# Routing's steps behind the passes that begin a pair of chunks, and the logits' products one slot sooner

## The chip, the cores and the metric

The kernel runs on one core of a Trainium2 chip. The metric is the time of one execution on the device in microseconds (us); the time of a kernel is the median of several executions. The engines are called as in the profile: PE (TensorE, matrix products), ACT (ScalarE), DVE (VectorE), POOL (GpSimd) and SP (here only a queue that issues DMAs). Each engine works through its own queue in order and waits on semaphores for the others.

## The reference

Three stages, each feeding the next; 2304 tokens (4 batches of 576) of 512 numbers.

```python
# 1. attention with a threshold, 8 heads of 64
scores = q @ k.T / 8
scores = where(scores >= max(scores) - tau, scores, -1e9)
x = softmax(scores) @ v
# 2. first mixture: a dense layer with a rational function
h = x @ w_in                                   # 512 -> 2048
P = a[0] + a[1]*h + a[2]*h**2 + a[3]*h**3
Q = 1 + abs(b[0])*abs(h) + abs(b[1])*h**2
x = (P / (Q + 1e-6)) @ w_out                   # 2048 -> 512
# 3. second mixture: 8 experts, the best one per token
logits = x @ w_gate
e = argmax(logits, axis=1)
gate = softmax(logits)[e];  eom = sigmoid(x @ w_output_gate)[e]
out = gate * eom * (relu(x @ w1[e]) @ w2[e])   # 512 -> 1024 -> 512
```

## The kernel before

The order of all engines' work is written out by hand: Python loops emit the instructions, and each engine runs its own in the order in which they were emitted.

**The first mixture** (`moe1`) works in slots. In slot `t` the chunk `c = t - 53` is begun: a chunk is 128 of the 2048 hidden columns for three token tiles of 128 (one of the six groups `r`). `emit_in(c)` issues its twelve products into PSUM (L945); two chunks, an even `c` and the odd one behind it, are a pair and share one PSUM tile `hps[p]`, of which there are two. So even `c` stand in odd slots and odd `c` in even slots. In a slot with odd `c` the pair that is complete is taken up by the vector engines, 768 columns at a time. ACT makes `ah` (L968), `s1` (L969) and `t1` (L970); POOL multiplies `t1` by `ah` (L971); DVE has two passes that begin the pair, L973 and L974, which read the pair's PSUM tile. In the next slot ACT makes the quotient as a logarithm and an exponential over the same PSUM tile (L980, L981). In the slot after that, DVE ends the pair with three passes, L959, L960 and L961, ACT writes `gh` (L998) and POOL `gl` (L999). Thus in each even slot DVE has the three last passes of one pair and then the two first of the next.

`emit_out` issues the nine products of the chunk begun five slots earlier with `w_out` (L1017); when a group has all its chunks, the rows are added up (L1047) and written out.

**Fillers.** `emit_in` is given a list `fill` of small pieces of work. `FILL = (0, 0, 9, 0, 0)` says how many of them are emitted behind each of the slot's DVE passes: up to nine behind the third. In a slot that both ends and begins pairs, they so stand between L961 and L973; what is left goes to the slot's end. The decoding of weights (`chains(t)`, until slot 93) and the steps of the first routing (`side.fill(t)`) both come in this list.

**The first routing** (`route(..., first=True)`) ranks the first nine token tiles by expert. It is a generator; each `yield` ends one step, mostly one small DVE instruction, some on ACT (L1446, L1455) or PE (counts L1326/L1328, permutation L1433, scales L1483). `ROUTE_STEPS` says how many steps each slot takes, from slot 127 to slot 152. Two parts of the first experts' work stand beside it: the halving of weights (L1650 on ACT, L1651 on DVE) and eight pieces of a transposition (L1598, L1601, L1602) in slots 141 to 148; L1602 is emitted at the end of a slot's passes ("late").

**The logits.** For a finished group of three tiles, `y_max` (L1071) and a power of two scale it, `y_hi` writes two halves of 16 bits (L1080 on ACT, L1081 on DVE), `y_turn` transposes them by DMA on SP (L1086), `y_logits` multiplies by the gates (L1096, eight products per tile, at the end of a slot's PE work), and `y_fin` (L1103 to L1108) writes the logits. Tile `i` is split and turned in slot `s + 1 + i`, multiplied in slot `s + Y_LOG + i`, and `y_fin` stands one slot behind the last product. The routing's PSUM results and the logits' products share one bank.

What follows the mixture is a loop over expert slots with a second routing in its beginning (`rt` in the names where the first has `temp`).

Of the kernel before, what the change touches and what calls it, by code (L numbers as in the profile page):

```python
# [105 lines left out]
Y_MAX = 0  # L106
Y_HI = 1
Y_TURN = 1
Y_LOG = 4
Y_FIN = 1  # L110
GATES = 44
ROUTE_AT = 9
# [554 lines left out]
def moe1(nc, tc, xT, vs, w_in, w_out, a, bb, w_gate, w_ogate, gates, ident, yd, part, L, consts, keep, side, early_bank):  # L667
# [3 lines left out]
    def pool(name, bufs, **kw):  # L671
        return (psum if "space" in kw else ctx).enter_context(tc.tile_pool(name=name, bufs=bufs, reuse_waits="tile", **kw))
# [21 lines left out]
    def w_cols(lo, n):  # L694
        if n < 4:
            return w4[lo][:, :, n * P:(n + 1) * P]
        return (wih, wil)[lo][:, :, (n - 4) * P:(n - 3) * P]
# [6 lines left out]
    def open_wo():  # L704
        p = right(keep, "wo")
        wo.append([p.tile([P, NFC // 2, DM], F32R, name=x) for x in ("woh", "wol")])
# [4 lines left out]
    def at(slot, f, *args):  # L711
        hooks.setdefault(max(slot, 0), []).append((f, args))
# [3 lines left out]
    def chains(slot):  # L716

        return steps.pop(slot, [])

    def run(slot):  # L720
        order = (load_next, last_bits, exponent, sum_in, red_in, clamp_red, split_out, split_in, scale_in, factors_in)
        for f, args in sorted(hooks.pop(slot, ()), key=lambda x: order.index(x[0]) if x[0] in order else -1 - (x[0] in early)):
            f(*args)
# [137 lines left out]
    for key in STREAM:  # L861
        t = end[key]
# [9 lines left out]
    for m in GROUPS:  # L872
        if n < 2 * m:
            for i in range(n, n + m):
                at(end[0, i] + (i != 2), sum_in, i)
            t = SECOND_SUM if n else EARLY_SUM
# [6 lines left out]
        else:  # L883
            for i in range(n, n + m):
                at(end[0, i] + 1, sum_in, i)
            t = max(end[0, i] for i in range(n, n + m)) + 1
# [33 lines left out]
    def h_tile():  # L920
        return ps_h.tile([P, 2, DM], F32, tag="h", name="h")
# [8 lines left out]
    def buf(tag, bufs, dt=F32, name=None):  # L930
        return m_p.tile([P, 2, n], dt, tag=tag, bufs=bufs, name=name or tag)

    def emit_in(c, fill):

        p, odd = divmod(c, 2)
        ops, late = [], []
        if c < len(chunks):
            j, fc, r = chunks[c]
            t0 = TR * r
            if not odd:  # L940
                hps[p] = h_tile()
            hb = hps[p][:, odd]
            parts = [(0, k, lo) for k in range(4) for lo in range(2)] + [(1, k, 0) for k in range(4)]
            for i, (w, k, lo) in enumerate(parts):
                nc.tensor.matmul(  # L945
                    hb[:, 0:n], w_cols(w, fc)[:, k], xT[:, k, t0:t0 + TR, lo, :],
                    start=(i == 0), stop=(i == 11))
            if spare:
                first, last = spare.pop(0)(hb[:, n:DM])
                if first:  # L950
                    first()
                late.append(last)
        if odd:
            if p - 1 in st:
                q = p - 1
                t, s = st.pop(q)
                x = hps.pop(q)[:, :, 0:n]
                ops += [
                    lambda: stt(t, t, one, x, op0=ALU.add, op1=ALU.mult),  # L959
                    lambda: stt(x, t, 2.0, x, op0=ALU.subtract, op1=ALU.mult),  # L960
                    lambda: (stt(s, s, na0, x, op0=ALU.add, op1=ALU.mult), emit_g(q, s)),  # L961
                ]
            if c < len(chunks):

                hp = hps[p][:, :, 0:n]
                c1, c2, ca1, ca3 = (cvs[:, i, t0 // UT, fc - 1:fc] for i in range(4))
                ah, t1, s1 = buf("ah", 1), buf("t", 3), buf("s", 4)
                nc.scalar.activation(ah, hp, AF.Abs, scale=c1)  # L968
                nc.scalar.activation(s1, hp, AF.Identity, bias=na2, scale=ca3)  # L969
                nc.scalar.activation(t1, ah, AF.Identity, bias=b0, scale=b1)  # L970
                nc.gpsimd.tensor_tensor(t1, t1, ah, op=ALU.mult)  # L971
                ops += [
                    lambda: stt(s1, s1, c2, hp, op0=ALU.mult, op1=ALU.mult),  # L973
                    lambda: stt(s1, s1, ca1, hp, op0=ALU.add, op1=ALU.mult),  # L974
                ]
                st[p] = t1, s1
        elif p - 1 in st:

            x, t = hps[p - 1][:, :, 0:n], st[p - 1][0]
            nc.scalar.activation(x, t, AF.Ln, bias=one)  # L980
            nc.scalar.activation(x, x, AF.Exp, scale=-1.0)  # L981
        ops += late
        if c == 1:
            at(HALVES[0] + 0.5, lambda ops=ops: [f() for f in ops])
            ops = []
        fill = list(fill)
        for f, k in itertools.zip_longest(ops, FILL):
            if f:
                f()
            for _ in range(min(k or 0, len(fill))):  # L990
                fill.pop(0)()
        for f in fill:
            f()

    def emit_g(q, s):

        gh, gl = buf("t", 3, F32R, "gh"), buf("s", 4, F32R, "gl")
        nc.scalar.activation(gh, s, AF.Copy)  # L998
        nc.gpsimd.tensor_tensor(gl, s, gh.bitcast(F32), op=ALU.subtract)  # L999
        for i in range(2):  # L1000
            gs[2 * q + i] = gh[:, i], gl[:, i]
# [4 lines left out]
    def emit_out(c):  # L1006
        j, fc, r = chunks[c]
        gh, gl = gs.pop(c)
        _, (f0, f1), end = SEGS[j]
        first, last = fc == f0, fc == f1 - 1  # L1010
        if first:
            for i in range(TR):
                acc[r, i] = bank(i)
        wh, wl = (x[:, fc % (NFC // 2)] for x in wo[fc // (NFC // 2)])
        for i in range(TR):
            for m, (g, w) in enumerate(((gh, wh), (gh, wl), (gl, wh))):
                nc.tensor.matmul(  # L1017
                    acc[r, i], g[:, i * P:(i + 1) * P], w, start=first and m == 0, stop=last and m == 2)
        if last:
            for i in range(TR):  # L1020
                (part_out if end == 1 else y_out)(r, i)
# [128 lines left out]
    for r in ORDER:  # L1150
# [3 lines left out]
        else:  # L1154
            at(s + Y_MAX, y_max, r)
            for i in range(TR):
                at(s + Y_HI + i, y_hi, TR * r + i)
                at(s + Y_TURN + i, y_turn, TR * r + i)
                at(s + Y_LOG + i, y_logits, TR * r + i)
            at(s + Y_LOG + TR - 1 + Y_FIN, y_fin, r)  # L1160
            s += TR
# [11 lines left out]
    for t in range(PRE, START + len(chunks) + G_LAG):  # L1173
        if t == END:
            open_wo()
            open_wo()
            d2_p.append(pool("d2", 1))
            ps_b.append(pool("ps_b", 1, space=PSUM))
            nc.sync.dma_start(out=gates[:, :, 0:E], in_=w_gate.rearrange("(k p) e -> p k e", p=P))
            nc.sync.dma_start(out=gates[:, :, E:2 * E], in_=w_ogate.rearrange("(k p) e -> p k e", p=P))  # L1180
            run(t - 0.5)
        c = t - START
        fill = chains(t) + side.fill(t)
        if 0 <= c < len(chunks) + 2:
            emit_in(c, fill)
        else:
            for f in fill:
                f()
        if G_LAG <= c < len(chunks) + G_LAG:
            emit_out(c - G_LAG)  # L1190
        if len(chunks) <= c < len(chunks) + UN:
            side.first_products(c - len(chunks), half_tile)
        if t in hooks:
            run(t)
        if t < END:
            yield
        for x in ((0.5,), (0.75, 0.8)) if t in HALVES else ():
            for y in x:
                run(t + y)
            yield  # L1200
# [624 lines left out]
def kernel(ctx, tc, q, k, v, tau, w_in, w_out, a, b, w_gate, w_ogate, w1, w2, out):  # L1825
    nc = tc.nc
    with tc.manual_schedule():
# [22 lines left out]
        experts = Experts(ctx, nc, tc, yd, L, rt, R, w1, w2, ident, out, xT)  # L1850
        bank = []
        gen = moe1(nc, tc, xT, vs, w_in, w_out, a, b, w_gate, w_ogate, gates, ident, yd, part, L,
                   lambda tmp: routing_constants(nc, main, tmp, R), ctx, experts, bank)
        attention(nc, tc, q, k, v, tau, xT, vs, ident, gen, bank)
# [36 lines left out]
```

## Time and profile before

| | |
|---|---|
| median of three executions | 1012.47 us (1008.74 to 1013.61) |
| the profiled execution's own time | 1013.9 us |
| its span, first to last instruction | 1011.9 us |
| mean granted TensorE clock | 0.979 |
| PE busy | 935.0 us (92%) |
| DVE busy | 795.1 us (79%) |
| ACT busy | 679.8 us (67%) |
| POOL busy | 540.8 us (53%) |

Times in the rows below are counted from the span's first instruction. The attention fills about the first 325 us, the first mixture the time from there to about 760 us, the experts the rest. A line of a timeline gives an instruction's start and length, its engine, source line and operation, what it writes and reads, and in brackets the idle time of its engine just before it and what ended that. The length of an instruction counts from its issue, so one that had to stand still shows it as length.

### The profile page before, as it was taken

To read this page: it belongs to the slowest core of one execution; us is meant where nothing else is said; L and a number is where in the kernel's file an instruction comes from. 1 tells how busy PE (TensorE), PEld (TensorE's weight loads), DVE (VectorE), ACT (ScalarE), POOL (GpSimd) and SP (SyncE) were. 2 spreads that over 40 slices of the span, in tenths; PEclk is the share of its full clock that TensorE was granted. 3 is DMA by queue.
4 is the path that set the end of the run, shared out by engine and by line. 5 is a ranking of instruction groups with operands and counts; after the bars stand their busy time and mean duration, and the time that the engine had idled before them with its cause. 6 is when DMAs were issued, how large, how long until landed. Compare 5 with 4: busy or idle time off the path is not lost. (4 is left out here: it accounts for less than half of the span.)

```text
span 1011.9 us, 20733 instructions
## 1 busy us (share of the span) xinstructions
PE 935.0 (92%) x7899; PEld 685.9 (68%) x7899; DVE 795.1 (79%) x1337; ACT 679.8 (67%) x1006; POOL 540.8 (53%) x540
## 2 busy tenths in 40 slices
PE   8898899999988899988999999988789999999996
PEld 5565566666656566655666666655468999999995
DVE  5888889999988897977777878989983986565652
ACT  5788788888887687878766666665553454555551
POOL 2587788889884497788845443435331132111220
PEclk9999999999989899999999999999998999999998
DMA  8999999999996333321012212051113021111340
GB/s 211 161 196 217 200 188 193 195 192 210 183 184 168 134 115 115 115 68 69 1 33 62 73 52 63 32 134 34 46 50 135 22 64 42 43 42 43 124 131 21
DMA packets 234188, 110.26 MB, mean 109 GB/s; under 512 B 196832, under 2 KB 221408, under 8 KB 234080
## 3 DMA queue, kind: packets, MB, share of 16 engines
q1 hardware_dynamic: 230816, 98.89, 44.7%
q0 software_dynamic: 3120, 9.96, 3.0%
q8 instruction: 64, 1.05, 0.4%
q14 instruction: 44, 0.36, 0.1%
q10 hardware_dynamic: 144, 0.00, 0.0%
HBM read 82.61 MB, written 13.63 MB: 95 GB/s over the span
## 5 line engine op out<-in xcount | busy, mean ns | idle before, releaser
L387 POOL TENSOR_TENSOR php<-e,php 128x512 f16<-128x512 f32 x144 | 166.7, 1162 | 66.5 <-ACT php L385 66.0
L971 POOL TENSOR_TENSOR t<-t,ah 128x768 f32<-128x768 f32 x48 | 87.9, 1830 | 177.5 <-ACT t L970 174.6
L945 PE MATMUL h<-xT,wih 128*128 128x384 f16 x768 | 143.6, 331 | 31.1 <-DVE s L961 22.5
L945 PEld LDWEIGHTS <-wih 128*128 128x128 f16 x768 | 68.4, 98 | 94.8 <-DVE s L961 28.7
L1017 PE MATMUL acc<-woh,gh 128*128 128x512 f32 x288 | 126.8, 440 | 1.8 <-ACT part L1034 1.7
L369 ACT ACTIVATE e<-s,mn 128x576 f32<-128x576 f32 x144 | 107.1, 744 | 31.4 <-DVE mn L368 27.9
L357 PE MATMUL s<-kt,qT 64*128 64x256 f32 (+3 forms) x640 | 118.3, 459 | 8.8 <-DVE mn L374 7.9
L381 DVE SCALAR_TENSOR_TENSOR e<-s,mn,e 128x576 f32<-128x576 f32 x144 | 116.2, 807 | 5.3 <-ACT e L369 5.2
L1718 POOL DMA_INDIRECT out_dram<-os,sidx x19 | 24.1, 1268 | 179.8 <-ACT os L1717 150.1
L1017 PE MATMUL acc<-wol,gh 128*128 128x512 f32 x288 | 115.1, 400 | 1.9 <-POOL wol L857 1.9
L1017 PE MATMUL acc<-woh,gl 128*128 128x512 f32 x288 | 114.6, 398 | 1.9 <-POOL gl L999 1.9
L415 PEld LDWEIGHTS <-pt 128*128 128x128 f16 (+1 forms) x2240 | 78.5, 101 | 53.5 <-issue 50.2
L368 DVE TENSOR_REDUCE mn<-s 128x1 f32<-128x576 f32 x144 | 107.6, 747 | 8.3 <-PE s L357 8.2
L385 ACT ACTIVATE php<-e 128x576 f16<-128x576 f32 x144 | 98.6, 685 | 4.8 <-DMA pt<-php 2.8
L999 POOL TENSOR_TENSOR gl<-s,gh 128x768 fp32r<-128x768 f32 x48 | 91.0, 1897 | 7.0 <-issue 4.6
L415 PE MATMUL xps<-vs__112,pt 128*128 128x65 f16 (+1 forms) x2240 | 92.9, 196 | 0.0
L980 ACT ACTIVATE h<-t,co 128x768 f32<-128x768 f32 x48 | 43.5, 906 | 68.6 <-POOL t L971 25.2
L945 PE MATMUL h<-xT,wil 128*128 128x384 f16 x384 | 80.6, 334 | 0.0
L959 DVE SCALAR_TENSOR_TENSOR t<-t,co,h 128x768 f32<-128x768 f32 x48 | 48.5, 1010 | 34.0 <-POOL gl L999 21.1
L968 ACT ACTIVATE ah<-h,cvs 128x768 f32<-128x768 f32 x48 | 43.3, 902 | 42.5 <-PE h L945 39.0
L1651 DVE TENSOR_TENSOR wol<-xT,woh 128x1024 fp32r<-128x1024 f32 x45 | 56.8, 1270 | 13.5 <-ACT woh L1650 13.5
L1017 PEld LDWEIGHTS acc<-woh,gh 128*128 128x128 f32 x288 | 55.2, 192 | 16.2 <-ACT part L1034 2.1
(390 smaller groups left out, 2321.1 us busy)
## 6 DMA issues: line engine op xcount, KB each, us to landing
xT<-in_moe_w_dram SPq DMA_DIRECT2D x80, 512.0 KB
raw<-in_moe_w_in_dram SPq DMA_DIRECT2D x16, 512.0 KB
raw<-in_moe_w_out_dram SPq DMA_DIRECT2D x16, 512.0 KB
yd<-y SPq DMA_DIRECT2D x18, 256.0 KB
raw<-in_k_dram SPq DMA_DIRECT2D x16, 256.0 KB
raw<-in_q_dram SPq DMA_DIRECT2D x16, 256.0 KB
xT<-in_v_dram SPq DMA_DIRECT2D x8, 512.0 KB
part<-part SPq DMA_DIRECT2D x15, 256.0 KB
```

What stands on the lines that cost most here:

```text
L357: nc.tensor.matmul(ps[po:po + m, o:o + n], qT[r, g % 2, hh, t, po:po + m], KT[g][r, bb, c:c + n], start=True, stop=True)
L368: nc.vector.tensor_reduce(mn[:, n:n + 1], st[i], axis=AX.X, op=ALU.min)
L369: nc.scalar.activation(e[:, n], st[i], AF.Exp, bias=mn[:, n:n + 1], scale=-1.0)
L381: nc.vector.scalar_tensor_tensor(e[:, n], st.pop(i), mn[:, 2 + n:3 + n], e[:, n], op0=ALU.is_le, op1=ALU.mult)
L385: nc.scalar.activation(hi, e[:, n], AF.Copy)
L387: nc.gpsimd.tensor_tensor(lo[:, b:b + 512], e[:, n, a:a + 512], hi[:, a:a + 512], op=ALU.subtract)
L415: nc.tensor.matmul(x, pt[:, blk, po:po + m], vv[:, par, hh, j, :], start=False, stop=(i % 6 == 5 and n == 13))
L945: nc.tensor.matmul(hb[:, 0:n], w_cols(w, fc)[:, k], xT[:, k, t0:t0 + TR, lo, :], start=(i == 0), stop=(i == 11))
L971: nc.gpsimd.tensor_tensor(t1, t1, ah, op=ALU.mult)
L999: nc.gpsimd.tensor_tensor(gl, s, gh.bitcast(F32), op=ALU.subtract)
L1017: nc.tensor.matmul(acc[r, i], g[:, i * P:(i + 1) * P], w, start=first and m == 0, stop=last and m == 2)
L1651: (self.nc.gpsimd if pool else self.nc.vector).tensor_tensor(cut(lo), src, cut(hi).bitcast(F32), op=ALU.subtract)
```

## The change

The list of fillers is parted. The decoding's pieces stay where they were, behind the third pass; the routing's steps come in a list of their own, `rest`, which is emitted behind all passes of the slot (and behind L1602 where there is one). Only slots that both end and begin pairs differ by that: the even slots from 128 to 148. In them, routing's steps stood between L961 and L973 and now stand behind L974. Besides, `Y_LOG` goes from 4 to 3, so that each tile's products with the gates, and `y_fin`, come one slot sooner.

```diff
-Y_LOG = 4
+Y_LOG = 3
...
-    def emit_in(c, fill):
+    def emit_in(c, fill, rest):
...
         for f, k in itertools.zip_longest(ops, FILL):
             if f:
                 f()
             for _ in range(min(k or 0, len(fill))):
                 fill.pop(0)()
-        for f in fill:
+        for f in fill + rest:
             f()
...
-        fill = chains(t) + side.fill(t)
+        fill, rest = chains(t), side.fill(t)
         if 0 <= c < len(chunks) + 2:
-            emit_in(c, fill)
+            emit_in(c, fill, rest)
         else:
-            for f in fill:
+            for f in fill + rest:
                 f()
```

## Rows read from the trace of the kernel before

**Rows 1.** Stretches: busy time by engine, granted clock, DMA share, GB/s.
```profile
637.00:757.00 120.00, 104.85 (x592) 71.58 (x590) 108.22 (x174) 69.71 (x91) 47.89 (x26) 0.97 0.22 62
...
680.00:692.00 12.00, 9.43 (x56) 5.97 (x55) 10.05 (x14) 6.27 (x8) 3.89 (x2) 0.86 0.32 102
```

**Rows 2.** What PE waited for, 626 to 757 us: total, times, longest.
```profile
PE h L945 <- DVE wol L1602: 6.2, 2, 4.1
PE h L945 <- DVE s L961: 5.5, 5, 2.2
```

**Rows 3.** Timeline of POOL, slots 128, 130 and 134.
```profile
646.78 1.83 POOL L971 TENSOR_TENSOR t<-t,ah 128x768 f32<-128x768 f32 x1 [4.47 <-ACT t L970]
...
655.26 1.85 POOL L971 TENSOR_TENSOR t<-t,ah 128x768 f32<-128x768 f32 x1 [4.84 <-ACT t L970]
657.07 1.84 POOL L999 TENSOR_TENSOR gl<-s,gh 128x768 fp32r<-128x768 f32 x1
...
673.38 1.81 POOL L971 TENSOR_TENSOR t<-t,ah 128x768 f32<-128x768 f32 x1 [6.30 <-ACT t L970]
675.16 1.84 POOL L999 TENSOR_TENSOR gl<-s,gh 128x768 fp32r<-128x768 f32 x1
```

**Rows 4.** Timeline of DVE, slot 134.
```profile
673.44 1.79 DVE L1404 CAST temp<-temp 128x9 int32<-128x9 f32 x1
675.26 1.76 DVE L1406 TENSOR_SCALAR temp<-temp 128x9 int32<-128x9 int32 x1
```

**Rows 5.** L1406's instructions: ns minimum/median/maximum, first and last start.
```profile
L1406 DVE TENSOR_SCALAR rt<-rt x1: 175/175/175, 797.5 to 797.5; 128x18 int32<-128x18 int32 x1
```

**Rows 6.** Timeline of DVE, slots 128 to 132.
```profile
645.56 0.22 DVE L1323 TENSOR_TENSOR temp<-temp 128x72 f16<-128x72 f32 x1
...
645.77 1.01 DVE L973 SCALAR_TENSOR_TENSOR s<-s,cvs,h 128x768 f32<-128x768 f32 x1
...
654.04 0.17 DVE L1342 CAST temp<-temp 128x8 f32<-128x8 int32 x1
...
655.32 1.01 DVE L973 SCALAR_TENSOR_TENSOR s<-s,cvs,h 128x768 f32<-128x768 f32 x1
...
657.30 1.86 DVE L1071 TENSOR_REDUCE ymax<-y 128x1 f32<-128x512 f32 x3
...
661.23 1.01 DVE L959 SCALAR_TENSOR_TENSOR t<-t,co,h 128x768 f32<-128x768 f32 x1
```

**Rows 7.** Timeline of PE: beginnings of slots, and the routing's products.
```profile
641.79 1.48 PE L945 MATMUL h<-xT,wih 128*128 128x384 f16 x8
...
647.80 0.20 PE L1326 MATMUL acc<-temp,upper 128*128 128x80 f16 x1
...
664.34 1.47 PE L945 MATMUL h<-xT,wih 128*128 128x384 f16 x8 [1.76 <-DVE temp L1380]
...
684.46 2.10 PE L945 MATMUL h<-xT,wih 128*128 128x384 f16 x8 [2.21 <-DVE s L961]
...
688.34 0.24 PE L1433 MATMUL acc<-temp 128*128 128x8 f16 x3 [0.36 <-DVE temp L1427]
...
722.64 2.69 PE L945 MATMUL h<-xT,wih 128*128 128x384 f16 x8 [4.08 <-DVE wol L1602]
...
734.99 1.46 PE L945 MATMUL h<-xT,wih 128*128 128x384 f16 x8 [2.17 <-DVE wol L1602]
```

**Rows 8.** Timeline of ACT, slot 135.
```profile
679.50 0.91 ACT L980 ACTIVATE h<-t,co 128x768 f32<-128x768 f32 x1 [5.11 <-DVE temp L1415]
```

**Rows 9.** Timeline of DVE, slots 136 and 144.
```profile
684.32 3.97 DVE L1427 TENSOR_TENSOR temp<-row,temp 128x384 f16<-128x384 f16 x2
...
728.56 1.01 DVE L973 SCALAR_TENSOR_TENSOR s<-s,cvs,h 128x768 f32<-128x768 f32 x1 [1.30 <-ACT s L969]
```

**Rows 10.** One stretch of 1 us, and PE's first product of the fourth group's logits.
```profile
670.00:671.00 1.00, 1.00 (x7) 0.82 (x5) 1.00 (x2) 0.45 (x1) 0.00 (x0) 1.00 0.58 104
...
672.45 0.36 PE L1096 MATMUL acc<-g,mag 128*128 128x32 f16 x8
```

## The prediction, made before the changed kernel ran

> **What bounds the kernel now.** I read the stretches first. The ten slots whose steps move lie between 637 and 757 us of the span: PE is busy 104.85 of 120 us there, DVE 108.22 [rows 1]. Both are nearly full, and the kernel moves on with PE's chunks; so what a slot loses shows as PE waiting, 15 us here. Next came what PE waits for in that stretch [rows 2]: 11.7 us in seven waits at the start of a chunk, five on L961 (it is the last read of a pair's PSUM tile, and the pair after next needs that tile) and two on L1602; an eighth, of 1.76 us at 664.34, is put down to the step right behind L961 [rows 7]. The reader is to see that all of them end on DVE, whose queue is in order: a routing step costs PE time by where it stands in that queue.
>
> Then I laid POOL's and DVE's timelines side by side. After each second chunk POOL runs two passes, L971 and L999, back to back, 1.8 us each [rows 3]. In slot 134 the step L1404 starts at 673.44 and ends at 675.23, as L971 ends (675.19); L1406 starts at 675.26 and ends at 677.02, as L999 ends (677.00) [rows 3, 4]. In the second routing, with no POOL pass beside it, L1406 took 0.175 us on twice the elements [rows 5]. So a tiny step that reads only SBUF stands still while a POOL pass runs; one gets through at each seam. The passes L973 and L974, which read PSUM, kept their 1.0 us beside POOL [rows 3, 6].
>
> [...]
>
> **Where the moved steps land.** In slot 128 the second chunk starts at 641.79 [rows 7], L971 runs from 646.78, 5.0 us later, and L999 behind it takes 1.84, so that it ends at about 650.4, 8.6 us later [rows 3]. ACT lets L973 begin 4.0 us after the chunk's start (645.77 [rows 6]), and L973 with L974 take 1.98 us (655.32 to 657.30 [rows 6]). So behind the passes a step starts no sooner than 5.9 us after the chunk: always inside POOL's two passes. Where DVE was early, the steps ran free before and will now be held; where it was late, they were held already, and now the two passes use that time. Thirty-four DVE and two ACT instructions move, in ten slots; no work is added or removed, no DMA moves, and PE's own order changes only for the products. SP's weight loads wait for the expert numbers (L1377, L1387) and POOL's gathers for L1439; both are issued two slots or more behind these steps, which cover the lateness.
>
> **The steps, slot by slot** (lateness of PE against the profiled execution, clock falls aside):
>
> Slot 128, L1323. It ran at 645.56, before POOL [rows 6]. Now it starts at 645.77 + 1.98 = 647.75, is held to 648.61 and ends at 648.8. PE's count (L1326) wants it at 647.80 [rows 7] and blocks the output products behind it. **+1.0 us**; 0.25 if it isn't held, 2.6 if it misses the seam (650.4 less 647.80). I take 1.0: both of slot 134's steps caught theirs.
>
> Slot 130, seven steps. They took 654.04 to 655.32, ending as L971 began at 655.26 [rows 3, 6]. Now the passes run 654.2 to 656.2, L1342 is held to 657.1, L1345 to 658.9, and with 1.1 us for the rest the end is 660.0, not 657.30 where L1071 begins [rows 6]. DVE has no idle from there to L959 at 661.23 [rows 6], and PE already waits 1.76 us for that L961 [rows 7]; so all of it reaches PE. **+2.7**; nil if not held, 3.0 if the POOL pass itself starts later.
>
> Slots 132 and 134. In 132 nothing is won, one hold taking the place of another: -0.1. In 134 the hold (1.79 + 1.76 us [rows 4]), which stood ahead of the passes, now hides them: DVE is free some 2 us sooner, and ACT's logarithm no longer waits 5.11 us for L974 [rows 8]. PE's wait of 2.21 at 684.46 [rows 7] is what that can give back. **-2.3** with 132; between 0 and -3.
>
> Slot 136, L1427 twice. They took 3.97 us from 684.32, held at both seams [rows 9], and PE waited 0.36 for them (688.34 [rows 7]). Now they start behind the passes and end 0.4 us after L999, at 690.5, while PE, 1.4 late, gets there at 687.7. It waits 2.8 us and goes on at 690.6 instead of 688.34. Lateness goes from 1.4 to 2.3: **+0.9** (0 to 2).
>
> Slot 138, L1444 and ACT's L1446. L1444 was free; now it is held to L971's end, and L1446, which needs it, stands in ACT's queue ahead of the next logarithm. **+0.65** (0.3 to 1.5). Slot 140: a step held once, before as after; nil.
>
> Slot 142. Like 134: two held steps before the passes, and PE's 4.08 us wait at 722.64 behind them [rows 7]. The passes move under the hold. **-1.8** (0 to -2).
>
> Slot 144. Four steps of 0.5 us ran in the 1.30 us in which DVE waited for ACT [rows 9]; that cover goes, they stand behind the passes and meet L971 and L999, ahead of the weight split. **+1.1** (0.5 to 2). Slot 148: 0.5 us in such a wait; POOL's later pass hides it, nil.
>
> **Products a slot sooner.** PE does as many. The tightest is the second tile of a group: its transposition is still moving in the stretch 670 to 671, and the product would stand where the first tile's is now, at 672.45 [rows 10]: some 1 us to spare, so nil (up to 1 us if the later DVE eats it). The product shares its PSUM bank with the routing's counts and may wait for L1394 there; a few tenths at most. The four steps of the logits' end move past the routing's DVE reads of slots 137 and 149: same time, 0 to 0.4 either way. Outside the routing's slots all such waits are covered: products and transpositions have a slot between them.
>
> **Clock.** Behind the wait of 2.21 us the eight matmuls took 2.10 us and not 1.47, behind that of 4.08 us 2.69, behind 1.76 us 1.47 [rows 7]. [...] Mine has waits of about 4.5 (slot 133), 2.8 (137) and 2.3 us (144); I count two falls again, so nil, with two more (+3.4) or two fewer (-3.4) as ends.
>
> **Sum.** 1.0 + 2.7 - 2.3 + 0.9 + 0.65 - 1.8 + 1.1 = 2.25 us later. What follows the mixture is PE at full load, so the shift goes through to the end: 1013.9 + 2.3 = 1016.2 us against the profiled execution, whose time stands 1.4 us over the median shown. Against the median: 1012.5 + 2.3 = **1014.8 us**, +0.2%.
>
> **Rivals.**
> *The clock falls more often* (slower). PE's new waits at 133 and in 136/137 each cost a fall besides those the kernel already has: 2.25 + 3.4 = 5.7 us, 1018.1; with the missed seam in slot 128 (+1.6), 1019.7. For: 4.5 us is longer than any wait that brought a fall here. Against: a wait of 2.17 us at 734.99 brought none [rows 7], and slow products partly stand where DVE is late anyway. Decides from the second added fall on.
> *Slot 130 isn't held* (faster). If its steps slip in ahead of POOL, or a POOL pass yields, 2.7 and 0.75 of the first term go: -1.2. PE then waits under 2 us in 133, and the waits at 684.46 and 722.64 shrink below those that brought a fall: -3.4 more; slot 144's 1.1 goes too: -5.7, 1006.8. For: those steps are 0.2 us each and in the kernel before they just got through. Against: the seam lies where two of three rows would be held. It decides at slot 130: L1342 under 0.3 us.
> *It doesn't matter* (no change): gains and holds cancel as they stand; -1 to +1 us, 1011.5 to 1013.5. This is inside my forecast's own range.
>
> **Chances.** Half a percent, 5 us, is about what a measurement of this kernel tells from no change. The forecast, -2 to +5 us (1010.5 to 1017.5), with the third rival in it: 0.57. The clock rival and other longer waits: 0.28. The unheld rival: 0.15. The range reaches to both, 1007.5 to 1020.5. Faster 0.15, same 0.57, slower 0.28.
>
> **What would show it.** In the changed profile: L1323 stretched to about 1 us and a PE wait before L1326; L1342 and L1345 at 1 and 1.8 us and a PE wait over 4 us a little later; L1404 and L1406 no longer delaying L973; a wait of 2 to 3 us before L1433; the wait that was 4.08 us near 2.3. The prediction is wrong if L1342 is short, if the wait at 133 is under 2.5 us, or if more than three stretches at half clock stand between 640 and 760 us.

## The result and the profile after

The changed kernel takes 1013.88 us (median of twelve executions, 1011.6 to 1020.6), the kernel before 1008.95 us (twelve, 1004.7 to 1013.6): the ratio is **1.0051, 95% interval 1.0032 to 1.0070**. It is slower by 4.9 us, at the edge of the half percent that I had drawn as the bound. The forecast was 2.3 us and no clear change, within -2 to +5 us: 4.9 is just inside. That the time itself lies well inside 1010.5 to 1017.5 is luck in part, for the kernel before takes 3.5 us less over twelve executions than the median of three from which I had counted.

The two profiled spans don't show it: 1011.7 us after, 1011.9 before. The 4.9 us are hidden because in this execution slot 128 begins at 635.67 us, and in that of before at 641.79 [rows 7]. Of these 6.1 us, 4.6 are there already at the first product of the first mixture (297.9 and 302.5 us), ahead of all that the change touches. Some 0.6 are the change's own, which I had overlooked: the products with the gates come sooner for the earlier groups too. Counted from slot 104, the six profiled kernels with `Y_LOG = 3` reach slot 128 0.6 to 0.7 us sooner than the kernel before, the three others with 4 do not (0.1 to 0.2 later). Every lateness below is counted from the start of slot 128 in the same execution, and does not include these 0.6 us.

What PE waited for in the changed kernel, 631 to 751 us (total, times, longest; compare [rows 2]):

```profile
PE h L945 <- DVE s L961: 6.8, 4, 4.3
PE h L945 <- DVE wol L1602: 5.3, 2, 2.9
PE acc L1433 <- DVE L L1107: 3.1, 1, 3.1
PE acc L1326 <- DVE temp L1323: 0.8, 1, 0.8
```

The list has what the prediction asked for: a wait before the counts, one over 4 us, one of 3 us before the permutation, and the wait that was 4.08 us at 2.9. The total went from 13.9 us (the waits of [rows 2], the 1.76 and the 0.36 of [rows 7]) to 16.0.

The same stretch (columns as in [rows 1]), and a part of it:

```profile
631.00:751.00 120.00, 104.13 (x573) 70.41 (x572) 103.23 (x167) 67.86 (x89) 46.67 (x26) 0.94 0.22 62
...
685.00:692.00 7.00, 6.12 (x24) 3.96 (x24) 4.23 (x10) 0.00 (x0) 0.00 (x0) 0.53 0.00 0
```

The granted clock is 0.94 against 0.97 in [rows 1]. In stretches of 1 us it is 1.00 but for 661 to 665, 685 to 693 and 733 to 737, where it goes down to 0.50; the output products behind the permutation came every 0.43 us at 0.50 and not every 0.23 us as at 1.00. An estimate of what the clock takes from a stretch is its length multiplied by 1 less the mean: 0.06 x 120 = 7.2 us against 3.6 (6.8 against 3.4, added up from stretches of 1 us). By this estimate the 3.4 us between the two are the larger part of what this execution is late at slot 148, 5.2 us.

Timeline of DVE, slots 128 and 130 (compare [rows 6]):

```profile
641.65 0.92 DVE L1323 TENSOR_TENSOR temp<-temp 128x72 f16<-128x72 f32 x1
...
651.04 0.90 DVE L1342 CAST temp<-temp 128x8 f32<-128x8 int32 x1
651.98 1.82 DVE L1345 TENSOR_TENSOR temp<-temp,low 128x64 f32<-128x64 f32 x1
...
654.65 1.86 DVE L1071 TENSOR_REDUCE ymax<-y 128x1 f32<-128x512 f32 x3
```

Timeline of POOL, slot 130:

```profile
650.08 1.84 POOL L971 TENSOR_TENSOR t<-t,ah 128x768 f32<-128x768 f32 x1 [5.79 <-ACT t L970]
651.86 1.85 POOL L999 TENSOR_TENSOR gl<-s,gh 128x768 fp32r<-128x768 f32 x1
```

L1342 and L1345, 0.17 and 0.23 us before, end at 651.94 and 653.80, to a tenth as L971 (651.92) and L999 (653.71) end. Timeline of PE: the counts, slots 133, 137, 138, 144 and 146, and the permutation (compare [rows 7]):

```profile
642.62 0.20 PE L1326 MATMUL acc<-temp,upper 128*128 128x80 f16 x1 [0.77 <-DVE temp L1323]
...
661.70 2.74 PE L945 MATMUL h<-xT,wih 128*128 128x384 f16 x8 [4.30 <-DVE s L961]
...
680.68 1.47 PE L945 MATMUL h<-xT,wih 128*128 128x384 f16 x8 [0.43 <-DVE s L961]
...
685.88 0.38 PE L1433 MATMUL acc<-temp 128*128 128x8 f16 x9 [3.07 <-DVE L L1107]
686.12 0.77 PE L1017 MATMUL acc<-woh,gh 128*128 128x512 f32 x1
...
690.11 2.51 PE L945 MATMUL h<-xT,wih 128*128 128x384 f16 x8
...
721.21 1.46 PE L945 MATMUL h<-xT,wih 128*128 128x384 f16 x8 [2.86 <-DVE wol L1602]
...
732.42 2.03 PE L945 MATMUL h<-xT,wih 128*128 128x384 f16 x8 [2.41 <-DVE wol L1602]
```

The eight matmuls behind the 4.30 us took 2.74 us and not 1.47; behind the 3.07 us the output products (0.63 us each and not 0.39 to 0.40) and the next slot (2.51) were slow too; behind 2.41 us the eight took 2.03, behind 2.86 us 1.46.

### The profile page after: what moved, and what is told of

It is laid out like the page before. It is cut to its first block, busy times and chain, and to the rows that moved or that the text cites. A ratio compares the mean times of both kernels' runs of the same rounds, so it can differ in the third digit from the quotient of the medians.

```text
span 1011.7 us, 20732 instructions
## 1 busy us (share of the span) xinstructions
PE 931.7 (92%) x7899; PEld 683.9 (68%) x7899; DVE 793.1 (78%) x1337; ACT 679.6 (67%) x1006; POOL 540.7 (53%) x540
## 5 line engine op out<-in xcount | busy, mean ns | idle before, releaser
L971 POOL TENSOR_TENSOR t<-t,ah 128x768 f32<-128x768 f32 x48 | 87.9, 1831 | 180.3 <-ACT t L970 178.2
L357 PE MATMUL s<-kt,qT 64*128 64x256 f32 (+3 forms) x640 | 115.5, 450 | 9.4 <-DVE mn L374 8.4
L999 POOL TENSOR_TENSOR gl<-s,gh 128x768 fp32r<-128x768 f32 x48 | 91.2, 1900 | 7.4 <-issue 4.7
```

What stands on the lines that cost most here:

```text
L357: nc.tensor.matmul(ps[po:po + m, o:o + n], qT[r, g % 2, hh, t, po:po + m], KT[g][r, bb, c:c + n], start=True, stop=True)
```

## The experiments

Eight kernels. The table is worked out from the timelines of PE, one execution of each kernel: how much later (+) or sooner (-) a slot starts than in the kernel before, in us, each execution counted from its own start of slot 128.

```
slot            133     135     137     138     141     144     146     148
changed        +3.5    +4.3    +2.3    +5.6    +6.8    +4.7    +3.6    +5.2
order alone    +3.5    +3.9    +1.9    +4.1    +4.4    +2.3    +2.8    +4.4
products al.    0.0     0.0     0.0    +4.4    +5.3    +1.6    -0.1    -0.1
held slots      0.0     0.0    -2.4    -4.2    -4.2    -6.3    -8.0    -8.0
not 130        +2.6    +4.7    +2.7    +5.4    +5.9    +3.8    +3.8    +3.7
not 128, 130    0.0    -0.7    -2.7    -1.3    -1.1    -3.2    -2.6    -1.0
POOL idle 130  +1.2    +0.4    -1.6    +1.3    +1.6    -0.5    -0.3    -0.3
held and 136    0.0     0.0    -2.3    +0.4    +0.4    -1.8    -2.1    -2.1
busy 133       +3.4    +2.7    +0.7    +3.1    +4.0    +1.8    +1.4    +1.4
```

**Order alone** (from the changed kernel):

```diff
-Y_LOG = 3
+Y_LOG = 4
```

> Only the new order of the routing's steps; products where they were. Mine: the order makes most of the loss. In the changed kernel the permutation products (L1433) waited 3.07 us, the last 0.5 of it for L1107 of the logits' end, which now stands in DVE's queue in front of slot 137; with that back, L1433 waits for L1427 and about 2.5 us. 3 to 5 us over before, ratio 1.003 to 1.005. Rival, the earlier products make the loss: 1.000 to 1.001.

Measured: 1.0055 (1.0033 to 1.0076). The order makes the whole loss. L1433 waited 2.3 us in two pieces, for L1427, as expected. There is one wait that I hadn't seen, which the earlier products avoid in the changed kernel. It is that of PE's first product of the last tile, in slot 148:

```profile
756.28 0.35 PE L1096 MATMUL acc<-g,mag 128*128 128x32 f16 x8 [2.57 <-DVE temp L1495]
```

L1495 reads the same PSUM bank, and now stands behind the passes of that slot; this 2.57 us comes after the slots of the table. Most of it is given back: PE's next wait, for L1698, is 3.40 us in the changed kernel (at 757.89) and 1.41 here (at 766.74).

**Products alone**:

```diff
         fill, rest = chains(t), side.fill(t)
+        fill, rest = fill + rest, []
```

> Only the products and the logits' end one slot sooner; routing's steps between the passes as before. Mine: not free. L1433 writes the PSUM bank that the logits' end (L1106, L1107) reads; that end now stands behind L974 of slot 136, so L1433 waits to about 690.8 instead of 688.3 of the trace before: 2 to 4 us over before with a fall of the clock, ratio 1.002 to 1.004. Rival, as I predicted, the earlier products and the end are hidden: 0.9995 to 1.0005.

Measured: 0.9997 (0.9984 to 1.0010). My expectation of a loss fell; the time I predicted, nil, held. The wait is there:

```profile
PE acc L1435 <- DVE L L1107: 4.2, 1, 4.2
```

(L1435 is L1433 of the other kernels.) With half clock behind it (0.50 over 688 to 694) it makes slot 138 4.4 us late. But DVE is as far on as it would have been, and PE's next waits shrink. That of slot 144 is 0.97 us and not 4.08, and slot 146 begins 0.1 us early:

```profile
721.33 1.46 PE L945 MATMUL h<-xT,wih 128*128 128x384 f16 x8 [0.97 <-DVE wol L1604]
```

So this wait of 4.2 us cost nothing in the end (ratio 0.9997): PE would otherwise have waited for DVE a little later.

**Held slots alone**:

```diff
-Y_LOG = 3
+Y_LOG = 4
...
         fill, rest = chains(t), side.fill(t)
+        if t not in (134, 140, 142):
+            fill, rest = fill + rest, []
```

> Products as before; routing's steps go behind the passes only in the slots where POOL held them already (134, 140, 142). Mine, the hold by POOL's passes decides by slot: the waits of 2.2 and 4.1 us at slots 137 and 144 shrink to under 1 and about 2, no new wait at 133, one or two falls of the clock less: 4 to 8 us under before, ratio 0.992 to 0.996. Rival, a hold removed in one slot comes back in the next: 0.999 to 1.001.

Measured: **0.9952 (0.9927 to 0.9977), 1003.86 us: faster than both kernels.** PE's waits in that stretch, up to slot 148:

```profile
PE h L945 <- DVE wol L1604: 4.8, 2, 2.8
...
PE h L945 <- DVE s L961: 2.7, 3, 1.5
PE h L945 <- DVE last L1384: 1.8, 1, 1.8
```

Timeline of DVE, slots 134 and 136 (L1406 is L1404, L1429 is L1427 of the other kernels):

```profile
671.31 1.01 DVE L974 SCALAR_TENSOR_TENSOR s<-s,cvs,h 128x768 f32<-128x768 f32 x1
672.24 1.62 DVE L1406 CAST temp<-temp 128x9 int32<-128x9 f32 x1
673.90 0.17 DVE L1408 TENSOR_SCALAR temp<-temp 128x9 int32<-128x9 int32 x1
...
678.45 1.02 DVE L1429 TENSOR_TENSOR temp<-row,temp 128x384 f16<-128x384 f16 x2
```

The passes use the time of the hold, only one step is still held (1.62 us), and DVE gets to slot 136 so early that its two steps, left between the passes, run free: 1.02 us and not 3.97 [rows 9]. The waits at slots 137 and 144, for which I had expected under 1 and about 2 us, are nil and 2.8. No wait is left before the permutation, and the granted clock of the stretch is 0.99:

```profile
634.00:754.00 120.00, 107.42 (x624) 76.02 (x623) 103.46 (x175) 71.22 (x93) 51.36 (x28) 0.99 0.24 69
```

The profiled execution gains 8.0 us up to slot 148; the ratio is 4.8 us, the medians (1003.86 and 1009.32) 5.5 apart. Over all executions the mean granted clock of both kernels is 0.983, so the clock doesn't make this gain. Its executions spread from 998.5 to 1009.5 us, more than those of the kernel before (1004.7 to 1013.1).

**Slot 130 back**:

```diff
         fill, rest = chains(t), side.fill(t)
+        if t == 130:
+            fill, rest = fill + rest, []
```

> The changed kernel with slot 130's seven steps back between the passes. Mine: L1342 and L1345 run free again, the wait at slot 133 goes from 4.3 us to under 2 and the clock doesn't fall there: 4 us less than the changed kernel, about +1 us against before, ratio 1.000 to 1.002. Rival, slot 130 only moves the wait: like the changed kernel, 1.004 to 1.006.

Measured: 1.0053 (1.0032 to 1.0074). Missed: the time is as without it, and the wait at slot 133 is 3.44 us. The rows of DVE tell why (L1360 is L1358, the last of slot 130's steps):

```profile
653.10 0.16 DVE L1344 CAST temp<-temp 128x8 f32<-128x8 int32 x1
...
654.29 1.76 DVE L1360 SCALAR_TENSOR_TENSOR lim<-temp 128x8 f32<-128x8 f32 x1
```

and one of POOL:

```profile
654.19 1.83 POOL L971 TENSOR_TENSOR t<-t,ah 128x768 f32<-128x768 f32 x1 [5.80 <-ACT t L970]
```

Six of seven steps run free; the last meets POOL's pass by 0.1 us and is held to its end. In the kernel before the next pass, L973, could start 0.06 us behind L971's start [rows 3, 6]: the step, begun at 655.24, had just got through in 0.17 us. Slot 128 still behind its passes had put DVE behind POOL by that tenth.

**Slots 128 and 130 back** (`t in (128, 130)` in the edit above):

> The changed kernel with the steps of slots 128 and 130 back between the passes (in the run with only 130 back, L1323's hold had left DVE late, and the last of 130's steps was held for 1.76 us). Mine: both run free, the wait at slot 133 is 1.8 us again, the clock doesn't fall there, and slot 137 then gains as in the run with the held slots alone: slot 138 at -1 to +1 us of the kernel before, later waits as in the changed kernel: ratio 0.997 to 1.001. Rival, the loss sits in the permutation's wait and not in 128 and 130: 1.004 to 1.006.

Measured: 0.9999 (0.9978 to 1.0019), 4 to 5 us less than the changed kernel; slot 133 waits 1.75 us, slot 137 begins 2.7 us early, and the permutation with its wait of 3.07 us then takes half of that back (slot 138 at -1.3). The clock doesn't fall behind that wait; rows of PE, and a stretch (columns as in [rows 1]):

```profile
658.95 1.47 PE L945 MATMUL h<-xT,wih 128*128 128x384 f16 x8 [1.75 <-DVE s L961]
...
681.57 0.37 PE L1435 MATMUL acc<-temp 128*128 128x8 f16 x9 [3.07 <-DVE L L1107]
```

```profile
678.00:692.00 14.00, 10.93 (x64) 7.53 (x61) 10.57 (x17) 6.19 (x8) 5.64 (x4) 1.00 0.01 4
```

In the changed kernel the same wait of 3.07 us had 7 us at 0.53 behind it, so a wait's length alone doesn't tell whether the clock falls. The loss sits in these two slots and what follows from them; no run has slot 128 alone back.

**POOL idle in slot 130** (from the changed kernel):

```diff
-                nc.gpsimd.tensor_tensor(t1, t1, ah, op=ALU.mult)
+                if c != 77:
+                    nc.gpsimd.tensor_tensor(t1, t1, ah, op=ALU.mult)
...
-        nc.gpsimd.tensor_tensor(gl, s, gh.bitcast(F32), op=ALU.subtract)
+        if q == 37:
+            nc.scalar.activation(gl, s, AF.Copy)
+        else:
+            nc.gpsimd.tensor_tensor(gl, s, gh.bitcast(F32), op=ALU.subtract)
```

> The changed kernel, in which POOL does nothing in slot 130: for that pair the product of t1 with ah is left out, and the lower half is written by ACT as a copy. The order on DVE is the changed one. Mine, POOL's passes hold the steps: L1342 and L1345 take under 0.3 us each (0.90 and 1.82 in the changed kernel), the wait at slot 133 goes from 4.3 to about 2 us. Rival, the place behind the passes itself is slow: lengths and wait as they were.

One profile. L1342 and L1345 are L1346 and L1349 there:

```profile
652.34 0.17 DVE L1346 CAST temp<-temp 128x8 f32<-128x8 int32 x1
652.54 0.23 DVE L1349 TENSOR_TENSOR temp<-temp,low 128x64 f32<-128x64 f32 x1
```

In the same place behind the passes, with no POOL pass beside them (POOL is idle for 14.01 us, until 659.57), they take 0.17 and 0.23 us, against 0.90 and 1.82; the wait at slot 133 is 1.97 us, and slot 133 begins 2.3 us sooner than in the changed kernel:

```profile
660.67 1.48 PE L945 MATMUL h<-xT,wih 128*128 128x384 f16 x8 [1.97 <-DVE s L961]
```

The hold is POOL's.

**Held slots and 136** (`t not in (134, 136, 140, 142)`, `Y_LOG = 4`):

> The kernel with the held slots (134, 140, 142), and slot 136 behind the passes too. Mine: L1427 is then held twice, L1433 waits 2 to 3 us in slot 137, slot 138 is 2 to 4 us later than with the held slots alone, and a good part stays: ratio 0.996 to 1.000 against before. Rival, DVE is late anyway and the later waits take it up: as with the held slots, 0.993 to 0.997.

Measured: 0.9988 (0.9972 to 1.0004). The permutation is cut into three by L1427's three instructions (the first stands in slot 135 and isn't moved), and PE waits 2.7 us:

```profile
686.25 0.23 PE L1435 MATMUL acc<-temp 128*128 128x8 f16 x3 [0.84 <-DVE temp L1429]
688.33 0.23 PE L1435 MATMUL acc<-temp 128*128 128x8 f16 x3 [1.85 <-DVE temp L1429]
```

With the slowed products behind it (every 0.43 us and not 0.23), slot 138 is 4.6 us later than with the held slots alone (+0.4 against -4.2), and slot 148 is still 5.9 us later. Moving those two instructions takes back most of the gain (the two intervals just touch).

**PE kept busy ahead of slot 133** (a zero column, and products by it added to running sums):

```diff
+        nc.vector.memset(co[:, 14:15], 0.0)
...
             emit_out(c - G_LAG)
+        if t == 132:
+            for i in range(5):
+                nc.tensor.matmul(
+                    acc[1, i % TR][:, 0:n], co[:, 14:15].to_broadcast([P, P]), wo[0][0][:, 0, 0:n].bitcast(F32),
+                    start=False, stop=False)
```

> The changed kernel with five products by zero, added to running sums, at the end of PE's slot 132, so that PE works through most of its 4.3 us wait ahead of slot 133 (sums unchanged). Mine: the clock doesn't fall there, slot 133 takes 4.1 us and not 5.8. Rival, the clock falls without regard to that wait: 5.8 us again.

One profile. Slot 133 begins as late as in the changed kernel, and runs at full clock (1.00 over 656 to 670, against 0.76 over 661 to 668 in the changed kernel):

```profile
658.10 3.39 PE L1194 MATMUL acc<-woh,co 128*128 128x384 f32 x10
662.54 1.48 PE L946 MATMUL h<-xT,wih 128*128 128x384 f16 x8 [1.05 <-DVE s L962]
```

The eight matmuls take 1.48 us, the slot 4.26 and not 5.83. So 1.6 us of the changed kernel's loss there go with the lower clock; in this execution, with PE busy for 3.39 us of the same wait, it stayed at 1.00. At slot 148 this execution is 3.8 us less late than the changed one. Only 1.6 of that is slot 133; the rest is a shorter fall behind the permutation (the eight matmuls took 2.13 us, against 2.51) and none at slot 146 (1.46 against 2.03), less one at slot 144 that the changed kernel doesn't have (behind a wait of 3.26 us four matmuls took 1.46 us, against 0.81); and one execution doesn't show whether those follow from the added products.

## Why the prediction was right, and where its size was off

**POOL's hold on the moved steps: right.** Slot 128 was to cost 1.0 us and cost 0.93; slot 130 2.7, and cost 2.55. POOL idle in 130 shows the hold by itself (0.17 and 0.23 us, against 0.90 and 1.82), and 128 and 130 put back bring the kernel to 0.9999. In the rows the conversion L1342 and the two-input step L1345 end with POOL's passes (651.94 and 653.80, against 651.92 and 653.71). The reduction of L1453 didn't wait: it took its 0.23 us beside L999 (at 707.06, while L999 ran from 706.12 to 707.95), while L1457, an addition of a constant right behind it, took 0.78 us and ended at 707.97, with L999. That it all reaches PE was right too: the wait at 133 was to be about 4.5 us and is 4.30.

**The gains: right.** Slots 132 and 134 were to give 2.3 us and gave 2.9 (+5.26 at slot 134 to +2.34 at 137). But 0.9 of that is there at slot 135 already, and is slot 132's, for which I had written 0.1: the order alone and the kernel with 128 and 130 back have it too, and the held slots alone, which leave 132 as it was, gain nothing at 135. Slot 142 with 140 was to give 1.8, and gave 2.15 (+6.84 to +4.69). Slot 138 was to cost 0.65 and cost 0.8; slot 144 1.1, and cost 0.45 (+3.09 at slot 145 to +3.54 at 146).

**Slot 136: its wait right, its price not.** L1433 was to wait 2.8 us and waited 3.07. The last 0.5 of it is for L1107: the logits' end, moved ahead of the permutation by the other part of the change, reads the bank that the permutation writes. I had seen that shared bank for the products and not for `y_fin`. The step was to cost 0.9 us and cost 3.2 up to slot 138: 1.3 are there when the wait ends, and 1.9 are the half clock behind it (from L1433 to slot 138 it is 4.23 us, and was 2.34).

**The clock: the step that failed in size.** "I count two falls again, so nil" was wrong. The 3.4 us for two falls can be worked out from the trace before: 12 us at 0.86 around the wait of 2.21 us [rows 1] and 5 us at 0.66 around the end of that of 4.08 us are 1.7 us each, by the estimate of 1 less the mean (columns as in [rows 1]):

```profile
722.00:727.00 5.00, 4.36 (x16) 2.45 (x16) 4.82 (x15) 1.14 (x3) 0.00 (x0) 0.66 0.28 52
```

In the profiled execution the end that I gave for it (+3.4) is what came: by that estimate the stretch lost 6.8 us to the clock and not 3.4. Behind the wait of 4.30 us the clock fell (0.57 over 661 to 665), behind that of 3.07 us for longer (0.53 over 685 to 692), and behind that of 2.41 us at slot 146 a third time (0.57 over 733 to 737); only behind that at slot 144, 2.86 us, it didn't (1.00 over 721 to 724), against a fall there before. The sum of the steps is 2.25 without it and 5.65 with the 3.4 us; measured are 5.2 from slot 128 to 148, and 4.9 in the medians. The clock rival had 0.28, and for this execution its mechanism was the truer forecast, though the time is 1.0051 and not its 1.0056.

That one execution's 5.2 us agree with the medians is luck in part, for on average the clock takes less. What the clock can have taken from an execution I estimate as its time, multiplied by 1 less its mean granted clock. On average that is 20.1 us in the changed kernel's twelve executions, and 17.4 and 18.7 us in the two sets of 23 of the kernel before that ran beside the experiments (each mean good to 0.5 to 1 us). An estimate from these figures: the clock makes 1.4 to 2.7 us of the 5, and the waits themselves about 3, somewhat more than the 2.25 of the sum.

**The products a slot sooner: right, by another road.** Alone they cost nothing (0.9997), but not because the logits' end is free: it makes a wait of 4.2 us that a later wait gives back. Ahead of slot 128 they gain some 0.6 us, and in the new order they spare a wait of 2.57 us in slot 148, most of which PE's next wait takes back; I had counted neither. Order alone and both together can't be told apart in time (1.0055 and 1.0051).

**The faster rival** needed slot 130 unheld. Its condition failed, but its reasoning is what the held slots alone use, by leaving 130 alone.

Left open: what decides whether the clock falls behind a wait (2.86 us at slot 144 brought no fall and 2.41 us at 146 did; 3.07 us before the permutation brought one in the changed kernel and none with 128 and 130 back), and why the kernel with the held slots alone spreads more between executions.

## What to carry to other kernels

Where VectorE's small steps stood decided here what they cost: a conversion or an elementwise step of 0.2 us that works on SBUF alone and started beside a GpSimd pass ended with that pass (0.8 to 1.8 us in the rows above), while L973, which reads PSUM, kept its 1.01 us beside one [rows 3, 6]. Put such steps behind work that reads PSUM where they would be held anyway, leave them where they run free, and decide slot by slot from the two timelines side by side; here the same move is 0.5% slower in ten slots and 0.5% faster in three. And price a new wait of TensorE with the lower clock that may follow it (behind three of the changed kernel's four waits of over 2 us it went down to 0.50, for 1.7 to 3.4 us lost by the estimate above), unless a later wait shrinks by as much.

## What the runs showed that I had not expected

- One tenth decided a hold: the last step of slot 130 started 0.10 us after POOL's pass and took 1.76 us, where in the kernel before it started 0.02 us ahead of it and took 0.17; with slot 128 put back as well slot 133's wait fell from 3.44 to 1.75 us.
- With five products by zero, 3.39 us of PE's work in a wait of 4.3 us, the granted clock stayed at 1.00 in the one execution, and slot 133 took 4.26 us and not 5.83.
